# DMA transposes for the last two batches, with the pooled branch added on GpSimd, in an attention and phase-mixing kernel

## The chip, the core and the metric

The kernel runs on one core of a Trainium2 chip. The engines of the core work side by side, each through its own queue in program order: TensorE (PE in the profile) multiplies matrices, VectorE (DVE) and ScalarE (ACT) do elementwise work, GpSimd (POOL) does elementwise work and band masks, and SyncE (SP) issues the DMA transfers. Engines wait for each other through semaphores. The metric is the device time of one execution in microseconds (us); a profiled execution also has a span, from its first to its last instruction.

## The reference

Batch 8, 8 heads, 576 positions, head dimension 64. The attention result has two branches: a pooled one (means over 4 positions, full attention on 144, repeated 4 times) and a local one (a band of 7 positions). Their sum x (576 x 512 per batch) passes a phase-mixing layer.

```python
out_d = sm_attn(q_d, k_d, v_d)                    # q_d, k_d, v_d: means over 4 positions
out_up = np.repeat(out_d, factor, axis=2)
mask = np.abs(pos[:, None] - pos[None, :]) < factor
scores = np.where(mask, scale * np.matmul(q, k.transpose(0, 1, 3, 2)), -1000000000.0)
...
out_local = np.matmul(attn, v)
x = out_up + out_local                            # heads side by side: (B, 576, 512)

theta = x @ w_theta
zr, zi = x * np.cos(theta), x * np.sin(theta)
y = np.einsum('ts,bsd->btd', w_tok_r, zr) + np.einsum('ts,bsd->btd', w_tok_i, zi)
u = x + y
out = u + np.maximum(u @ w_ch, 0.0)
```

## The kernel before

The work of a batch is cut into steps. Each kind of step is a generator that runs over the batches, and each has a letter. The string ORDER (L80) is the program: the loop at L659 takes one letter after the other and lets its generator do its next step. `pin` (L639) then chains the instructions of every engine in just this order, so ORDER fixes each engine's queue, SP's too. No step is moved by anything else.

The steps of a batch, with their letters:

- L `load` (13): four DMAs of q, four of k (each two heads), five of v, into a staging pool of 15 buffers. C `cast` (13): the same to bf16, on GpSimd, for q of batch 0 on ScalarE (`CASTS`, L200). q_tm and k_tm have one buffer each.
- A `turns` (5, L271): for two head pairs of q and k, nine PE transposes each (L285) into a PSUM tile, two ScalarE copies (L287) into qT or kT and a VectorE sum over groups of four positions (L295); the fifth step pools v, with two small products on GpSimd (L310).
- S `scores` (7, L324): two steps of pooled scores, then five chunks of band scores: matmuls (L379), exponential on ScalarE (L387), and two band masks on GpSimd (L394, L396; for batch 0 PE adds a mask, L375).
- N `pooled_out` (3): the pooled branch's result and its transpose xdT. V `outputs` (5): the local branch's psloc (L451), divided by its sums on VectorE into tmp (L460; four buffers).
- T `transposes` (5, L477): four PE transposes of tmp (L487), then VectorE adds xdT, each value for four positions, and writes x transposed, xT (L490).
- H `phases` (5, L500): theta (psth, L507) and its cosine and sine on ScalarE (cs, three buffers, L512 and L513). The fifth step handles the last 64 positions in transposed form (zT, L527); z `z_turn` turns them by a DMA transpose (L535).
- Z `modulate` (4, L540): four PE transposes of xT (L546), then VectorE multiplies them with cs into z (L547).
- X `mix` (5): the matmuls over positions (psu L564, psut L570) and the addition of x (uT, L565). u `u_turn` (2): DMA transposes of uT (L580, L582). R `channels` (5): matmuls with w_ch (psr, L594). O `store` (5): the last elementwise step (osb, L616) and the output DMAs (L622, L625).

Some letters are for set-up: K constants, l and c loads and casts of the weights, W their transposes into WT (L253 copies each result on VectorE), and D, six matmuls on constants that nothing reads (wu, L261), placed in the first 45 us. PSUM is used as two tiles of two banks (`w2`) and four of one (`w1`), taken in turn. Loads, stores and DMA transposes all go through SP's queue.

Of the kernel before, what the change touches and what calls it, by code (L numbers as in the profile page):

```python
# [47 lines left out]
def kernel(  # L48
# [27 lines left out]
    def w1(name, dt=FP32):  # L76
# [1 line left out]


    ORDER = (  # L80
        "LKCLCLLCACLLLLLLKAKCCLLCCCLDKAAlLLlLCCDCSSSCCLLASSLNNLVVllllCllNcCLLVCcCTALLLLLTASCccCcTSCHVVcDTZCCC"
        "ATAHlllHlHZZcHSDZLlLLLLWlccCCCcASSccDzlNCCCSWWWSLNWWCCLLLLLLLLLClCSWCCCCCSWWVAXVANXAACXVXSLTTLLLSuAC"
        "CVSTHTVNHHNLTZZCACCVcLLLLccLcHCCHXzLCZLLSRLLROOZCCCuCLLLLLAARLLLARLSSXCCSCSOOXVVCCCCXSNCVSTAVTCCSROT"
        "ATATCCLLCSXSSHNuHNVXZZAALLCAVHHVCCHNRRzOSSTOCLLCCLLRORLOLLuSCCTZZTSSCHVXVTAHCCNNLXLLZTANAHHLCCVVLLCH"
        "XACACCSLLLLXVXCCzLRSLLLSLLLOTLLLTZZCCSCZATALLuLXSLSHHVNXVNZTXTCAACCCCHHCCHVSuXXRSSROOzCZVNTRRCCSSOOR"
        "AuOuSZZVXVVTTXTLLLSCSCCCHTVXZNAXAAHHVCCHNXZCAHASSRRuROONRuOOSSZTTRSVOzZRSSOTROHVVRRHRSSOOTXOHNTZXNZH"
        "HVXVXXZZzVNVXTTXTHTVHHuuRTRROROOOZZHHzXZZXRXOXXXXXuuRRuROORRuOORORRROOROOO"
    )

    staged = {}  # L90
# [6 lines left out]
    def load(b):  # L97

        for hh in range(4):
            for nm, src in zip("qk", (q, k)):  # L100
                nc.sync.dma_start(
                    out=stage(b, f"{nm}{hh}"),
                    in_=src[b, 2 * hh:2 * hh + 2].rearrange("h (p r) d -> (h p) (r d)", r=WR),
                )
                yield
        for c in range(NCH):
            nc.sync.dma_start(
                out=stage(b, f"v{c}")[0:KW[c], 0:DM].rearrange("p (h d) -> p h d", d=D),
                in_=v[b, :, KS[c]:KS[c] + KW[c], :].rearrange("h p d -> p h d"),
            )  # L110
            yield

    def cast(b):

        q_tm = work.tile([P, 2, WR, 2, D], BF16, tag="q_tm", bufs=1, name=f"q_tm{b}")
        k_tm = work.tile([P, 2, WR, 2, D], BF16, tag="k_tm", bufs=1, name=f"k_tm{b}")
        v_w = v_ws[b % 2]
        inputs[b] = (q_tm, k_tm, v_w)
        eng = CASTS.get(b, CASTS[None])
        for hh in range(4):  # L120
            for i, dst in enumerate((q_tm, k_tm)):
                eng[i](out=dst[:, hh // 2, :, hh % 2, :],  # L122
                       in_=staged.pop((b, f"{'qk'[i]}{hh}")).rearrange("p (r d) -> p r d", d=D))
                yield
        for c in range(NCH):
            eng[2](out=v_w[0:KW[c], c, :, 0:D],  # L126
                   in_=staged.pop((b, f"v{c}"))[0:KW[c], 0:DM].rearrange("p (h d) -> p h d", d=D))
            yield


# [66 lines left out]


    dve, act, gp = nc.vector.tensor_copy, nc.scalar.copy, nc.gpsimd.tensor_copy
    CASTS = {0: (act, gp, gp), None: (gp, gp, gp)}  # L200


    wth = wpool.tile([P, 4, DM], BF16, name="wth")
# [5 lines left out]
    def weight_loads():  # L209

        for i in range(2):
            wst = staged["w", f"th{i}"] = moep.tile([P, 1024], FP32, tag="ur", name=f"th{i}")
            nc.sync.dma_start(out=wst.rearrange("p (c e) -> p c e", c=2),
                              in_=moe_w_theta[256 * i:256 * i + 256, :].rearrange("(c p) e -> p c e", p=P))
            yield
        tail = staged["w", "tail"] = moep.tile([P, 2, S], FP32, tag="xT", bufs=2, name="tail")
        for ri, w in enumerate((moe_w_tok_r, moe_w_tok_i)):
            wst = staged["w", ri] = moep.tile([P, 4, S], FP32, tag="z", name=f"tok{ri}")
            for ct in range(5):
                nc.sync.dma_start(out=wst[:, ct, :] if ct < 4 else tail[0:OC[4], ri, :], in_=w[P * ct:P * ct + OC[ct], :])  # L220
                yield
        for i in range(4):
            nc.sync.dma_start(out=stage("w", f"ch{i}")[:, 0:DM], in_=moe_w_ch[P * i:P * i + P, :])
            yield

    def weight_casts():

        for i in range(2):
            gp(out=wth[:, 2 * i:2 * i + 2, :].rearrange("p c e -> p (c e)"), in_=staged.pop(("w", f"th{i}")))
            yield  # L230
        for ri in range(2):
            for ct in range(5):
                src = staged["w", ri][:, ct, :] if ct < 4 else staged["w", "tail"][0:OC[4], ri, :]
                (gp, dve)[ri](out=w_tm[ri][0:OC[ct], ct, :], in_=src)
                yield
        for i in range(4):
            gp(out=wch[:, i, :], in_=staged.pop(("w", f"ch{i}"))[:, 0:DM])
            yield

    def weight_turns():  # L240

        for j in range(9):
            ps = w1(f"wps{j}", BF16)
            for ct in range(5):
                rows = OC[ct]
                for ri in ((j % 2,) if j < 8 else (0, 1)):
# [3 lines left out]
                        in_=w_tm[ri][0:rows, ct, P * (j // 2):P * (j // 2) + n],  # L250
                        identity=ident[0:rows, 0:rows],
                    )
            nc.vector.tensor_copy(out=WT[:, j, :], in_=ps[:, 0:S])  # L253
            yield

    def warm_up():
# [9 lines left out]
    WARM = ORDER.count("D")  # L266


    parts = {}

    def turns(b):  # L271

        q_tm, k_tm, v_w = inputs[b]
        qT = work.tile([P, 4, S], BF16, tag="qT", name=f"qT{b}")
        kT = kTs[b % 2]
        qdT = work.tile([P, 4, SD], BF16, tag="qdT", name=f"qdT{b}")
# [3 lines left out]
        for j in range(4):  # L280
            n, i = j % 2, j // 2
            tm, To = ((q_tm, qT), (k_tm, kT))[n]
            ps = w2(f"pstr{n}{i}_{b}", BF16).rearrange("p k e -> p (k e)")[:, 0:WR * P]
            for r in range(WR):
                nc.tensor.transpose(out=ps[:, P * r:P * r + P], in_=tm[:, i, r, :, :], identity=ident)  # L285
            for a in range(2):
                act(  # L287
                    out=To[:, 2 * i + a, 0:S].rearrange("p (w r) -> p w r", r=WR),
# [6 lines left out]
                nc.vector.tensor_reduce(out=dst, in_=src, axis=AX.X, op=ALU.add)  # L295
            yield

        vd = vds[b % 2]
        psa, psb = w1(f"psva_{b}"), w1(f"psvb_{b}")
        for c in range(4):  # L300
            nc.tensor.matmul(out=psa[KP * c:KP * c + KP, :], lhsT=PU, rhs=v_w[:, c, :, 0:D],
# [21 lines left out]

    def scores(b):  # L324

        qT, kT, qdT, kdP = parts.pop(b)

        pd = pds[b] = work.tile([P, H + 2, SD], BF16, tag="pd", name=f"pd{b}")
        pms[b] = []

        scale = SCL / 16.0

        def pooled_scores(dst, hh):
# [32 lines left out]
        )  # L366
        yield

        for c in range(NCH):
            kw, qn = KW[c], QN[c]  # L370
            ps = w2(f"psS{c}_{b}")
# [69 lines left out]

    def outputs(b):

        v_w = inputs.pop(b)[2]
        for c in range(NCH):
            kw, qn, cnt = KW[c], QN[c], QC[c]
            ps = w2(f"psloc{c}_{b}")
# [1 line left out]
            for h in range(H):  # L449
# [7 lines left out]
            rl = work.tile([P, 2, 4], FP32, tag="rl", name=f"rl{c}_{b}")  # L457
            nc.vector.reciprocal(out=rl[0:cnt], in_=pv[0:cnt, :, :, 64])
            tmp = tmps[b, c] = work.tile([P, DM], BF16, tag="tmp", bufs=4, name=f"tmp{c}_{b}")
            nc.vector.tensor_tensor(  # L460
                out=tmp[0:cnt].rearrange("p (e j d) -> p e j d", e=2, j=4),
                in0=pv[0:cnt, :, :, 0:D],
# [14 lines left out]
    def transposes(b):  # L477

        xdT = xds.pop(b)
        xT = xTs[b] = moep.tile([P, 4 * S], BF16, tag="xT", bufs=2, name=f"xT{b}")  # L480
        xA, xB = parted(xT)
        for c in range(NCH):
            cnt = QC[c]
            ps = w1(f"xTps{c}_{b}", BF16)[:, 0:512].rearrange("p (e t) -> p e t", e=4)
            tmp = tmps.pop((b, c))
            for dc in range(4):
                nc.tensor.transpose(out=ps[:, dc, 0:cnt], in_=tmp[0:cnt, P * dc:P * dc + P], identity=ident[0:cnt, 0:cnt])  # L487
            for dst, lo, n in ((xA[:, :, QS[c]:QS[c] + cnt], 0, cnt),) if c < 4 else ((xA[:, :, QS[4]:MAIN], 0, MAIN - QS[4]), (xB, MAIN - QS[4], HALF)):
                m = (QS[c] + lo) // 4
                nc.vector.tensor_tensor(  # L490
                    out=dst.rearrange("p e (m j) -> p e m j", j=4),
                    in0=ps[:, :, lo:lo + n].rearrange("p e (m j) -> p e m j", j=4),
                    in1=xdT[:, :, m:m + n // 4].unsqueeze(3).to_broadcast([P, 4, n // 4, 4]),
                    op=ALU.add,
                )
            yield
# [3 lines left out]
    def phases(b):  # L500
# [3 lines left out]
        for c in range(4):  # L504
            th = w1(f"psth{c}_{b}")
            for dc in range(4):
# [1 line left out]
                    out=th, lhsT=xA[:, dc, P * c:P * c + P], rhs=wth[:, dc, :],  # L508
                    start=(dc == 0), stop=(dc == 3),
                )  # L510
            cs = css[b, c] = moep.tile([P, 2, DM], BF16, tag="cs", bufs=3, name=f"cs{c}_{b}")
            nc.scalar.activation(out=cs[:, 0, :], in_=th, func=AF.Sin, bias=pihc, scale=1.0)  # L512
            nc.scalar.activation(out=cs[:, 1, :], in_=th, func=AF.Sin, bias=0.0, scale=1.0)  # L513
            yield
# [25 lines left out]
    def modulate(b):  # L540

        (xA, xB), z = parted(xTs[b]), zs[b]
        for c in range(4):
            ps = w1(f"psxt{c}_{b}", BF16)[:, 0:DM]
            for dc in range(4):
                nc.tensor.transpose(out=ps[:, P * dc:P * dc + P], in_=xA[:, dc, P * c:P * c + P], identity=ident)  # L546
            nc.vector.tensor_tensor(  # L547
                out=z[:, 2 * c:2 * c + 2, :], in0=ps.unsqueeze(1).to_broadcast([P, 2, DM]),
                in1=css.pop((b, c)), op=ALU.mult,
            )  # L550
            yield

# [97 lines left out]
    def batches(steps):  # L650
        for b in range(B):
            yield from steps(b)

    sequences = dict(L=batches(load), C=batches(cast), A=batches(turns), S=batches(scores), N=batches(pooled_out),
                     V=batches(outputs), T=batches(transposes), H=batches(phases), Z=batches(modulate),
                     K=constants(), z=batches(z_turn), u=batches(u_turn), X=batches(mix), R=batches(channels), O=batches(store),
                     l=weight_loads(), c=weight_casts(), W=weight_turns(), D=warm_up())
    pin()
    for s in ORDER:  # L659
        next(sequences[s])  # L660
# [33 lines left out]
```

## Time and profile before

| What | Value |
|---|---|
| Median of 5 runs | 253.4 us (252.87 to 254.29) |
| The profiled execution's own time | 252.99 us |
| Its span | 251.3 us, 6875 instructions |
| Granted TensorE clock, mean | 0.992 |
| DMA: moved, mean | 49.23 MB, 196 GB/s |
| psu (L564): 288 matmuls | 66.9 us busy, 379 ns mean |
| PE transposes of q and k (L285): 144 each | 11.4 and 11.1 us busy |
| PE transposes of tmp (L487): 160 | 14.6 us busy |
| PE transposes of xT (L546): 128 | 11.0 us busy |
| VectorE addition of the pooled branch (L490): 48 | 25.2 us busy, 548 ns mean |
| Table loads on ScalarE | 16, of 1283 ns each |

How to read it: busy time of a group is the time in which at least one of its instructions ran, and "mean" is the length of one. Matmuls are pipelined, so the mean of one is longer than the distance from one to the next. Busy shares are over the whole span; the page also gives them in 40 slices, in tenths. An engine's idle time is shown with what released it.

### The profile page before, as it was taken

The page shows a single profiled execution, that of the slowest core. Times are in us where ns is not written, and L with a number is a line of the kernel's source. Part 1 is how long each engine was busy: PE and PEld are TensorE (multiplying, and loading weights), DVE is VectorE, ACT ScalarE, POOL GpSimd, SP SyncE. Part 2 cuts the span into 40 slices and gives each one's busy share as a digit, 9 for nine tenths or more (in the row PEclk, how much of TensorE's full clock was granted, in tenths as well). Part 3 has the DMA queues.
Part 4 walks back from the last instruction along what each step waited for, and adds up shares of the span by engine and source line. Part 5 has one row for each costly group of instructions (what it writes and reads, how often), then busy time and mean ns, then how long its engine had stood idle before and what let it go on. Part 6 is the DMA issues. An engine that isn't in the chain of part 4 may idle for free.

```text
span 251.3 us, 6875 instructions
## 1 busy us (share of the span) xinstructions
PE 231.2 (92%) x2746; PEld 141.5 (56%) x2746; DVE 193.0 (77%) x357; ACT 159.2 (63%) x245; POOL 152.4 (61%) x211
## 2 busy tenths in 40 slices
PE   0958899999999999979999999999999999999992
PEld 0524555665774567546666666556755556555540
DVE  3444898888898888998989896897989578674363
ACT  4664899645998489959687859547997931520000
POOL 2648663999899999936979953969089410000000
PEclk9997999999999999999999999999999999999999
DMA  6999999999996999449799994762454315041596
GB/s 226 290 297 393 258 225 319 253 230 342 181 182 188 326 189 268 128 118 263 191 352 187 284 255 116 202 131 49 83 181 129 102 24 95 3 167 35 104 263 208
DMA packets 81439, 49.23 MB, mean 196 GB/s; under 512 B 64896, under 2 KB 66944, under 8 KB 81408
## 3 DMA queue, kind: packets, MB, share of 16 engines
q1 hardware_dynamic: 81408, 48.81, 76.6%
q8 instruction: 21, 0.34, 0.6%
q14 instruction: 10, 0.08, 0.2%
HBM read 33.59 MB, written 9.44 MB: 171 GB/s over the span
## 4 chain that ended last, share of the span: by engine, by line
PE 79%; ACT 8%; DVE 4%; DMA 3%; issue 2%; POOL 1%; SPq 1%; DVEq 0%; POOLq 0%; ACTq 0%
PE psu L564 25%; PE psth L507 10%; PE psr L594 7%; PE pstr L285 5%; PE psS L379 5%; PE psloc L451 4%; PE psut L570 3%; PE xTps L487 3%; ACT qT L287 3%; PE psxt L546 3%; DMA out_dram<-osb 2%; ACT kT L287 2%; PE psnd L413 2%; DVE osb L616 2%; PE wu L261 2%
## 5 line engine op out<-in xcount | busy, mean ns | idle before, releaser
L564 PE MATMUL psu<-WT,z 128*128 128x512 bf16 x288 | 66.9, 379 | 0.0
L387 ACT ACTIVATE pm<-psS 128x1024 bf16<-128x1024 f32 (+1 forms) x40 | 38.1, 980 | 15.8 <-PE psS L379 15.6
L394 POOL TENSOR_SCALAR_AFFINE_SELECT pm<-pm 128x1024 bf16<-128x1024 bf16 (+1 forms) x35 | 36.8, 1051 | 12.1 <-ACT pm L387 12.1
L564 PEld LDWEIGHTS <-z 128*128 128x128 bf16 x288 | 26.5, 98 | 27.7
L396 POOL TENSOR_SCALAR_AFFINE_SELECT pm<-pm 128x1024 bf16<-128x1024 bf16 (+1 forms) x35 | 36.6, 1045 | 2.4
L594 PE MATMUL psr<-wch,uT 128*128 128x512 bf16 x128 | 30.7, 379 | 1.5 <-DVE osb L616 1.5
L507 PE MATMUL psth<-wth,xT 128*128 128x512 bf16 x128 | 31.6, 379 | 0.4 <-DVE xT L490 0.4
L565 DVE TENSOR_TENSOR uT<-psu,xT 128x512 bf16<-128x512 f32 x32 | 22.0, 687 | 12.2 <-PE psu L564 12.1
L512 ACT ACTIVATE cs<-psth,pihc 128x512 bf16<-128x512 f32 x32 | 22.6, 707 | 11.9 <-PE psth L507 6.9
L295 DVE TENSOR_REDUCE qdT<-qT 128x288 bf16<-128x1152 bf16 x16 | 21.6, 1351 | 10.6 <-ACT qT L287 10.5
L122 POOL CAST k_tm<-st_k 128x576 bf16<-128x576 f32 x32 | 21.5, 673 | 13.4 <-DMA st_k<-in_k_dram 12.9
L460 DVE TENSOR_TENSOR tmp<-psloc,rl 120x512 bf16<-120x512 f32 (+2 forms) x40 | 27.6, 691 | 1.4
L490 DVE TENSOR_TENSOR xT<-xTps,xdT 128x480 bf16<-128x480 bf16 (+3 forms) x48 | 25.2, 548 | 3.6 <-PE xTps L487 3.6
L126 POOL CAST v_w<-st_v 128x512 bf16<-128x512 f32 (+1 forms) x40 | 23.4, 614 | 5.0 <-DMA st_v<-in_v_dram 5.0
L287 ACT COPY qT<-pstr 128x576 bf16<-128x576 bf16 x32 | 19.0, 647 | 9.8 <-PE pstr L285 9.7
L616 DVE SCALAR_TENSOR_TENSOR osb<-psr,ur 128x512 f32<-128x512 f32 x32 | 21.2, 685 | 3.6 <-PE psr L594 3.1
L295 DVE TENSOR_REDUCE kdP<-kT 128x300 bf16<-128x1200 bf16 x16 | 22.3, 1397 | 2.0 <-ACT kT L287 1.9
L287 ACT COPY kT<-pstr 128x576 bf16<-128x576 bf16 x32 | 19.1, 655 | 6.7 <-PE pstr L285 6.7
L547 DVE TENSOR_TENSOR z<-psxt,cs 128x1024 bf16<-128x1024 bf16 x32 | 21.0, 681 | 1.8 <-PE psxt L546 1.5
L122 POOL CAST q_tm<-st_q 128x576 bf16<-128x576 f32 x28 | 18.9, 673 | 2.5 <-PE psS L379 1.5
L513 ACT ACTIVATE cs<-psth 128x512 bf16<-128x512 f32 x32 | 19.7, 616 | 0.0
L594 PEld LDWEIGHTS <-uT 128*128 128x128 bf16 x128 | 11.5, 98 | 13.5 <-issue 2.1
(86 smaller groups left out, 378.5 us busy)
## 6 DMA issues: line engine op xcount, KB each, us to landing
st_q<-in_q_dram SPq DMA_DIRECT2D x32, 288.0 KB, 5.2
st_k<-in_k_dram SPq DMA_DIRECT2D x32, 288.0 KB, 5.5
st_v<-in_v_dram SPq DMA_DIRECT2D x32, 256.0 KB, 6.4
out_dram<-osb SPq DMA_DIRECT2D x32, 256.0 KB, 2.4
st_v<-in_v_dram SPq DMA_DIRECT2D x8, 192.0 KB, 5.1
tok<-in_moe_w_tok_r_dram SPq DMA_DIRECT2D x4, 288.0 KB, 7.4
tok<-in_moe_w_tok_i_dram SPq DMA_DIRECT2D x4, 288.0 KB, 5.2
th<-in_moe_w_theta_dram SPq DMA_DIRECT2D x2, 512.0 KB, 5.8
```

The lines of the kernel that those rows point to most:

```text
L122: eng[i](out=dst[:, hh // 2, :, hh % 2, :], in_=staged.pop((b, f"{'qk'[i]}{hh}")).rearrange("p (r d) -> p r d", d=D))
L287: act(out=To[:, 2 * i + a, 0:S].rearrange("p (w r) -> p w r", r=WR), in_=ps.rearrange("p (r a w) -> p a w r", r=WR, a=2)[:, a],)
L295: nc.vector.tensor_reduce(out=dst, in_=src, axis=AX.X, op=ALU.add)
L387: nc.scalar.activation(out=pv, in_=ps[0:kw].rearrange("p e (j w) -> p (e j) w", w=P)[:, :, 0:qn], func=AF.Exp, scale=SCL,)
L394: nc.gpsimd.affine_select(out=pv, in_=pv, compare_op=ALU.is_ge, fill=0.0, base=off, pattern=[[0, 8], [-1, qn]], channel_multiplier=1)
L396: nc.gpsimd.affine_select(out=pv, in_=pv, compare_op=ALU.is_ge, fill=0.0, base=6 - off, pattern=[[0, 8], [1, qn]], channel_multiplier=-1)
L460: nc.vector.tensor_tensor(out=tmp[0:cnt].rearrange("p (e j d) -> p e j d", e=2, j=4), in0=pv[0:cnt, :, :, 0:D], in1=rl[0:cnt].unsqueeze(3) ...
L490: nc.vector.tensor_tensor(out=dst.rearrange("p e (m j) -> p e m j", j=4), in0=ps[:, :, lo:lo + n].rearrange("p e (m j) -> p e m j", j=4), ...
L507: nc.tensor.matmul(out=th, lhsT=xA[:, dc, P * c:P * c + P], rhs=wth[:, dc, :], start=(dc == 0), stop=(dc == 3),)
L564: nc.tensor.matmul(out=ps, lhsT=z[:, j, P * dc:P * dc + P], rhs=WT[:, j, 0:MAIN], start=(j == 0), stop=(j == 8))
L594: nc.tensor.matmul(out=psr, lhsT=uA[:, dc, P * c:P * c + P], rhs=wch[:, dc, :], start=(dc == 0), stop=(dc == 3),)
L616: nc.vector.scalar_tensor_tensor(out=osb[:, 0:P * n].rearrange("p (e d) -> p e d", d=P), in0=psr[:, 0:P * n].rearrange("p (e d) -> p e d", ...
```

## The change

In batches 6 and 7 (`DMA_QK`, `DMA_X`, `DMA_Z`):

- q and k are turned by four DMA transposes (`turn_qk`, letter q) of 128 x 1152 into staging buffers; the ScalarE copies then read those.
- tmp is turned by five DMA transposes (`turn_x`, letter t) of 128 x 512, also into staging buffers. The rows of tmp that a chunk does not fill are set to zero on GpSimd before. GpSimd, not VectorE, adds xdT.
- xT is turned by one DMA transpose of 128 x 2048 (`turn_z`, letter x), and the multiplication for z reads that.

In all batches: steps are cut finer (loads and casts of v, letters v and w; pooled v, B; pooled scores, Q, apart from the band scores, S; w_ch, h and g), cs has four buffers in place of three, five of the nine copies into WT are on ScalarE, v is always cast on GpSimd, and ORDER is another string.

```diff
-        "LKCLCLLCACLLLLLLKAKCCLLCCCLDKAAlLLlLCCDCSSSCCLLASSLNNLVVllllCllNcCLLVCcCTALLLLLTASCccCcTSCHVVcDTZCCC"
...
+        "KLLLLCCLLKKKLCALCvCvvCCCDvvLLwLLAALLAlvlllSSLwLSwwwVBCCCCQQVNNlllAVcNvvvCTTAcvcTllCCSSHHVVDTTlllALHc"
...
-    CASTS = {0: (act, gp, gp), None: (gp, gp, gp)}
+    CASTS = {0: (act, gp), None: (gp, gp)}
...
-            nc.vector.tensor_copy(out=WT[:, j, :], in_=ps[:, 0:S])
+            (act, dve)[j % 2](out=WT[:, j, :], in_=ps[:, 0:S])
...
+    DMA_QK, DMA_X, DMA_Z = (6, 7), (6, 7), (6, 7)
+
+    def turn_qk(b):
+
+        if b in DMA_QK:
+            q_tm, k_tm = inputs[b]
+            for j in range(4):
+                t = turned[b, j] = stg.tile([P, WR, P], BF16, tag="st", name=f"qk{j}_{b}")
+                nc.sync.dma_start_transpose(out=t, in_=(q_tm, k_tm)[j % 2][:, j // 2].rearrange("p r h d -> p (r h d)"))
+                yield
+
+    def turn_x(b):
+
+        if b in DMA_X:
+            for c in range(NCH):
+                t = turned[b, "x", c] = stg.tile([P, 4, P], BF16, tag="st", name=f"xt{c}_{b}")
+                nc.sync.dma_start_transpose(out=t, in_=tmps.pop((b, c)))
+                yield
+
+    def turn_z(b):
+
+        if b in DMA_Z:
+            xA, xB = parted(xTs[b])
+            t = turned[b, "z"] = moep.tile([P, 16, P], BF16, tag="xr", bufs=1, name=f"xr_{b}")
+            nc.sync.dma_start_transpose(out=t, in_=xTs[b][:, 0:4 * MAIN])
+            yield
...
-            ps = w2(f"pstr{n}{i}_{b}", BF16).rearrange("p k e -> p (k e)")[:, 0:WR * P]
-            for r in range(WR):
-                nc.tensor.transpose(out=ps[:, P * r:P * r + P], in_=tm[:, i, r, :, :], identity=ident)
+            if b in DMA_QK:
+                ps = turned.pop((b, j)).rearrange("p r w -> p (r w)")
+            else:
+                ps = w2(f"pstr{n}{i}_{b}", BF16).rearrange("p k e -> p (k e)")[:, 0:WR * P]
+                for r in range(WR):
+                    nc.tensor.transpose(out=ps[:, P * r:P * r + P], in_=tm[:, i, r, :, :], identity=ident)
...
+            if b in DMA_X:
+                lo = 96 if c < 4 else 64
+                nc.gpsimd.memset(tmp[lo:], 0.0)
...
+            if b in DMA_X:
+                ps = turned.pop((b, "x", c))
+            else:
...
+            adder = nc.gpsimd if b in DMA_X else nc.vector
...
-                nc.vector.tensor_tensor(
+                adder.tensor_tensor(
...
-            cs = css[b, c] = moep.tile([P, 2, DM], BF16, tag="cs", bufs=3, name=f"cs{c}_{b}")
+            cs = css[b, c] = moep.tile([P, 2, DM], BF16, tag="cs", bufs=4, name=f"cs{c}_{b}")
...
+            if b in DMA_Z:
+                ps = turned[b, "z"][:, c:16:4, :]
+            else:
...
-                out=z[:, 2 * c:2 * c + 2, :], in0=ps.unsqueeze(1).to_broadcast([P, 2, DM]),
-                in1=css.pop((b, c)), op=ALU.mult,
+                out=z[:, 2 * c:2 * c + 2, :].rearrange("p r (e d) -> p r e d", d=P),
+                in0=ps.unsqueeze(1).to_broadcast([P, 2, 4, P]),
+                in1=css.pop((b, c)).rearrange("p r (e d) -> p r e d", d=P), op=ALU.mult,
```

In the new ORDER the end of the program, from the first mixing step of batch 6 on, reads `XXTttTTuTTXHHRHxROOROuROZHZHRZzZOXXuXXXXuRuRROOOXRRRuOORRROOOORO`; before it read `XTTXTHTVHHuuRTRROROOOZZHHzXZZXRXOXXXXXuuRRuROORRuOORORRROOROOO`.

## The prediction

> **What bounds the kernel now.** I read the page's busy rows and slices first, then the chain of waits, then what TensorE (PE) waited for between 60 and 240 us.
>
> ```profile
> PE 231.2 (92%) x2746; PEld 141.5 (56%) x2746; DVE 193.0 (77%) x357; ACT 159.2 (63%) x245; POOL 152.4 (61%) x211
> ...
> PE   0958899999999999979999999999999999999992
> ...
> POOL 2648663999899999936979953969089410000000
> ...
> PE 79%; ACT 8%; DVE 4%; DMA 3%; issue 2%; POOL 1%; SPq 1%; DVEq 0%; POOLq 0%; ACTq 0%
> ```
>
> PE is above 90% from the sixth slice (6.3 us each) to the last but one; only the start and the end have holes. GpSimd (POOL) is empty from slice 34 on.
>
> ```profile
> PE psr L594 <- DVE osb L616: 1.5, 1, 1.5
> PE psloc L451 <- ACT qT L287: 0.5, 2, 0.4
> PE psS L379 <- ACT qT L287: 0.4, 1, 0.4
> PE psS L379 <- ACT kT L287: 0.3, 1, 0.3
> PE xTps L487 <- DVE osb L616: 0.2, 1, 0.2
> ```
>
> The columns are waiter, what it waited for, total us, times, longest. Five rows, 2.9 us in 180: for most of the span the end is set by how much PE has to do. A change that takes work from PE is paid in full, one that takes it from another engine is not, unless it makes PE wait.
>
> **PE: what goes.** Batches 6 and 7 lose the turns of q and k (per batch 4 steps of 9), of tmp (5 of 4) and of x (4 of 4). The groups' busy means (225, 216, 219 ns for one turn) overlap, so I take start-to-start times from the order of time on PE (start, length, engine, line):
>
> ```profile
> 55.76 0.67 PE L285 MATMUL pstr<-ident,q_tm 128*128 128x128 bf16 x9
> 56.26 0.67 PE L285 MATMUL pstr<-ident,k_tm 128*128 128x128 bf16 x9
> ...
> 63.39 0.38 PE L487 MATMUL xTps<-ident,tmp 120*128 120x120 bf16 x4
> 63.61 1.03 PE L507 MATMUL psth<-wth,xT 128*128 128x512 bf16 x4
> ...
> 221.30 0.61 PE L546 MATMUL psxt<-ident,xT 128*128 128x128 bf16 x8
> 221.75 1.03 PE L507 MATMUL psth<-wth,xT 128*128 128x512 bf16 x4
> ```
>
> Nine turns take 0.50 us (55.76 to 56.26), four of tmp 0.22, eight of x 0.45. Per batch 4 x 0.50 + 4 x 0.22 + 0.17 (the short chunk, 33.76 to 33.92) + 0.90 = 3.95, for two batches **7.9 us**. By the groups' busy totals (79, about 91 and 86 ns each) it would be 12.1; I choose 7.9, since the next group starts before the last one's modelled end.
>
> **A rule that speaks against it.** The Trainium skill, "VectorE: DVE Perf Modes", section "The three transpose paths", gives 390 ns for a 128x128 turn on TensorE and 1309 ns by DMA, and its rules take TensorE where the result may lie in PSUM. 144 blocks (72, 40, 32) at 0.92 more each would be 132 us lost, if each stood on the path. The trace differs in what counts: a block holds PE for 0.056 us, and a DMA turn holds PE for nothing. I go by the trace, and ask which DMA turn is waited for.
>
> **The DMA turns.** Twenty are added: 8 of 128x1152 (295 KB), 10 of 128x512 (131 KB), 2 of 128x2048 (524 KB). The trace has the second size as z (landing 2.4/2.6/7.4 us min/median/max) and the third as ur:
>
> ```profile
> L535 SPq DMA_TRANSPOSE z<-zT x8: 1191/1270/2965, 42.0 to 225.2; - x8
> ...
> DMA to landing us min/median/max: 2.4/2.6/7.4
> ```
>
> ```profile
> L580 SPq DMA_TRANSPOSE ur<-uT x8: 1317/2370/4905, 62.4 to 237.8; - x8
> ...
> DMA to landing us min/median/max: 4.3/4.5/7.0
> ```
>
> So 131 KB cost 1.3 us of SP and 2.6 to land, 524 KB 2.4 and 4.5; 295 KB lie between, some 3.4 to land. SP gains 8 x 1.7 + 10 x 1.3 + 2 x 2.4 = 31 us, the DMA engines 4.7 MB. Loads and stores queue behind a turn on SP: the q and k turns of 6 and 7 sit among the loads of 6 and 7, whose casts come over 10 us of PE later; from 200 to 240 us the DMA share is 0.16 to 0.49. Bounds 0 to 3 us, taken at 0 apart from the two places below.
>
> **GpSimd, VectorE and ScalarE.** The add L490 takes DVE 3 x 0.647 + 0.668 + 0.412 + 0.265 = 3.3 per batch; DVE loses 6.6, which PE does not see. On POOL the nearest row is vd at L310 (two inputs, 256 elements, median 614 ns, 2.4 ns each): 480 elements 1.15, a batch 5.5, two 11.0. The ten memsets of tmp rows lie between a 103 ns POOL memset and a 673 ns cast; I take 0.3, 3 us in all. POOL's order from the fourth band select of batch 6 to the last add of batch 6 holds the selects of six band steps (12.6), vd of 7 (1.2), one cast (0.6), memsets (0.9) and adds (5.5): 20.8 us. PE has 24.8 from that step to the fourth phase step of batch 6, which needs the add. It fits by 4 us, less the exponential (1.03) that POOL trails by. Each memset also stands before DVE's write of tmp in rows both touch; behind that wait are psu's evictions. Five of nine WT copies go to ACT (0.45 on DVE, 0.65 like the other copies): 3 us on an engine full from 30 to 40 us, 0 to +2 at the start. The copies L287 now read SBUF; nearest row 0.65 in PSUM, taken the same, 0 to +0.1 each.
>
> **The second rule, and the place where it costs.** The Trainium skill, "SBUF — State Buffer", section "Who interferes with whom": a VectorE instruction with two SBUF inputs contends with a GpSimd one that reads SBUF, and the later one is blocked until the other finishes. The multiply z (L547) now has two SBUF inputs. This trace has one such DVE operation, zT:
>
> ```profile
> 105.75 3.01 DVE L527 TENSOR_TENSOR zT<-xT,cst 128x512 bf16<-128x512 bf16 x1 [0.18 <-ACT cst L525]
> ```
>
> Beside POOL's back-to-back vd and casts it took 3.01 us instead of 0.43, and the PE wait of 1.5 us above follows it. By the rule a multiply waits out one POOL instruction (1.15 at most): 4 for batch 6 is 4.6. By this row it is 2.6 each, 10.3, since POOL got in again. At batch 7 POOL's queue is empty. Between 0 and 10.3 I take the rule's 4.6: POOL's order has three adds and a select beside the four. From the eviction X5.0 to psu X6.0, PE has some 14.3 us and DVE 10.3, so 4 are covered. In that stretch x6's turn also stands on the way: last add of batch 6, turn 4.5, four multiplies 2.7, together 7.2, against 6.8 of PE work from the fourth phase step to psu of batch 6. The uncovered 0.6 and 0.4, and half a us for POOL's trail: **+1.5 us**, bounds 0 and 6.
>
> **The end.** For batch 7, after its last psloc PE has psu and psut of 5 and psu of 6 (8.8), then phases, psr of 5 and the rest of 6 (10.9): 19.7 us to psu of 7. Beside it: tmp 1, turn issue and landing 3.9, add 0.9, x turn 4.5: 10.3, earlier than the fourth phase (14.8). After the tail phase (16.2): ACT to 17.9, zT 18.4, z's turn 21.0; its matmul is psu's ninth, at 21.4. No wait. The last stores keep their order: 0.
>
> **The start, and batches 0 to 5.** The same work in another order.
>
> ```profile
> 16.05 0.30 PE L335 MATMUL psSd<-qdT,kdP 64*128 64x144 bf16 x4 [1.94 <-DVE kdP L295]
> ...
> 17.27 0.59 PE L375 MATMUL psS<-band,ident 128*128 128x512 bf16 x2 [0.69 <-ACT pd L345]
> ```
>
> The band scores of batch 0 waited for the pooled ones (1.94 + 0.69); they now come first and need only kT, about 14.4. By 50 us ACT's phases and tables bind both orders, so I keep 1.0 of the 2.6: **-1.0**, bounds -3.5 and +3. The table changes between exponential and sine stay at 15. Moved loads count the same: v behind q and k. The cs buffers rise from 3 to 4, for four phases before the first multiply of batch 6.
>
> **Sum.** The profiled execution took 252.99 (span 251.3 and 1.7 around it): 252.99 - 7.9 - 1.0 + 1.5 = 245.6. The shown median is 0.4 above that execution: **246.0**.
>
> **Rivals.**
> - A, the waits don't come and the start gives its 3.5: 252.99 - 7.9 - 3.5 + 0.4 = 242.0. For it: PE waited little before. Against: ACT at 9.4 of 10 from 30 to 40 us.
> - B, POOL and DVE block each other as at 105.75: +6 at psu of batch 6 instead of 1.5, 250.5. For: that row. Against: the same operation at 182.05 took 0.42 with vd beside it.
> - C, slower: the turns land late. At 7.4 and 7.0 instead of 2.6 and 4.5, and an SP held 4.9 by a ur turn, batch 7's multiplies end at 25.7 instead of inside 19.7 (+6), and batch 6's at 1.5 + 4.8 + 2.5 = +8.8: 252.99 - 7.9 - 1.0 + 14.8 + 0.4 = 259.3. It decides once added waits pass 8.9. For: the queue's packets take 76.6% of the engines. Against: late in the trace that share is half or less.
> - That PE keeps the turns is excluded by the diff; that they cost nothing is what the 2.9 us of waits deny.
>
> **Chances.** Forecast 0.50, A 0.12, B 0.16, C 0.22. Runs spread so that 0.3% (0.76 us) can be told from no change. Of B 0.03 and of C 0.04 fall inside it: faster 0.75, same 0.07, slower 0.18. The range of the forecast alone is 243.5 to 248.5; 241.5 to 255 leaves out a little of A and most of C's far half.
>
> **What would show it.** Right: PE's matmul count down by 144, PE above 90% in the same slices, psu of batch 7 starting without a wait. Wrong: PE waiting for z before psu of batch 6 or 7 (B: z much longer than 0.68; C: z idle on a DMA turn), for xT on POOL before psth, or PE holes before slice 25, where only the order changed.

## The result, and the profile after

The changed kernel takes 251.98 us (median of 38 runs, 250.58 to 255.74) against 253.25 us for the kernel before (73 runs on the same chips, 252.30 to 255.16). The ratio is 0.9957, with a 95% interval of 0.9945 to 0.9969: 1.1 us faster, where 7.4 were forecast. Medians are of all runs; ratios leave out single slow ones, over 1.5% above the fastest of their kernel. The profiled execution took 251.82 us, 1.17 less than the one before.

The page of the kernel after, in the rows and slices that were shown of before (now 6.25 us a slice), with the shares of the chain of waits:

```profile
PE 225.1 (90%) x2602; PEld 135.9 (54%) x2602; DVE 185.0 (74%) x340; ACT 170.1 (68%) x250; POOL 167.4 (67%) x233
...
PE   0878799799999989999999999999769999999991
...
POOL 4538773996999999979679576996498972600000
PEclk9997999999999999999999999999988999999997
...
PE 69%; ACT 12%; POOL 6%; DVE 4%; DMA 4%; issue 2%; SPq 0%; DVEq 0%; ACTq 0%; POOLq 0%
```

PE has its 144 matmuls fewer. But slices 29 and 30, at 175 to 187 us, are now 7 and 6 tenths, and PEclk falls to 8 in slices 30 and 31. VectorE (DVE) lost 8.0 us of work; ScalarE (ACT) gained 10.9 and GpSimd (POOL) 15.0. The part of the chain on PE fell from 79% to 69%; ScalarE and GpSimd took it over.

The three longest of PE's waits between 60 and 250 us, kernel after (waiter, what it waited for, total us, times, longest):

```profile
PE psvb L347 <- POOL v_w L131: 2.2, 1, 2.2
PE psr L650 <- DVE uT L621: 1.4, 1, 1.4
PE psloc L496 <- DVE tmp L508: 0.5, 1, 0.5
```

All three are new. The first two lie in that hole. The third comes at 204.6 us, behind a write of tmp that VectorE could not start, because GpSimd had yet to zero the empty rows:

```profile
203.88 0.69 DVE L508 TENSOR_TENSOR tmp<-psloc,rl 120x512 bf16<-120x512 f32 x1 [1.53 <-POOL tmp L507]
```

None of the three is a wait for z or for a DMA transpose.

To place the loss I take the PE work that the program puts between two steps (start-to-start times, as in the prediction) from the time that PE took for it. The steps are the X steps; X4.3 is the fourth mixing step of batch 4, X5.0 the first of batch 5. In the kernels with the new order X5.0 is counted from the last matmul ahead of it (195.33 us; psu itself starts at 195.44), so that this matmul's 0.1 us is in neither the time nor the work. The table compares one execution of each kernel.

| Stretch | After minus before, us |
|---|---|
| PE work in all (222.9 to 214.9) | -8.0 |
| lost time up to X3.0 (20.9 to 19.8): start, new order | -1.1 |
| lost from X3.0 (133.8) to X4.3 (173.0) | +1.1 |
| lost from X4.3 to X5.0: 22.3 taken for 16.9 of work; before 24.4 for 24.3 | +5.3 |
| lost from X5.0 (195.3) to X5.3 (207.6) | +0.8 |
| the rest: end of the program (0.4), rounding | +0.7 |
| change of the span (251.3 to 250.1) | -1.2 |

The PE work saved is there, to 0.1 us of what was forecast. Most of it is lost again in one stretch, from 173 to 195 us, in which batch 6's scores, batch 7's turns and batch 4's last steps meet.

**What happens there.** The granted clock and the busy times of the engines, kernel after (stretch, us, busy us and instructions of PE, PEld, DVE, ACT, POOL, then PEclk, DMA share, GB/s):

```profile
170.00:180.00 10.00, 8.61 (x99) 4.77 (x98) 7.38 (x13) 9.32 (x12) 3.98 (x8) 1.00 0.94 154
180.00:190.00 10.00, 7.80 (x102) 4.66 (x100) 5.44 (x11) 3.95 (x6) 9.44 (x13) 0.83 0.70 184
```

First ScalarE is full and GpSimd stands still; ten us later it is the other way round. ScalarE's groups by form say what fills it (instructions, busy us, mean ns, idle time before them):

```profile
L328 ACT COPY kT<-pstr 128x576 bf16<-128x576 bf16 x24 | 14.4, 660 | 2.4 <-PE pstr L326 2.4
L328 ACT COPY qT<-pstr 128x576 bf16<-128x576 bf16 x24 | 14.2, 647 | 11.3 <-PE pstr L326 11.2
...
L328 ACT COPY kT<-qk 128x576 bf16<-128x576 bf16 x8 | 9.4, 1238 | 0.0
L328 ACT COPY qT<-qk 128x576 bf16<-128x576 bf16 x8 | 9.2, 1208 | 0.0
...
L507 POOL MEMSET tmp<- 32x512 bf16 x8 | 3.9, 520 | 0.2
...
L263 ACT COPY WT<-wps 128x576 bf16<-128x576 bf16 x5 | 3.2, 639 | 3.0 <-PE wps L258 3.0
```

One more row, of the kernel before: the casts of q of batch 0, which ScalarE reads from SBUF in order.

```profile
L122 ACT CAST q_tm<-st_q 128x576 bf16<-128x576 f32 x4 | 2.6, 678 | 2.3 <-DMA st_q<-in_q_dram 2.3
```

The same copy takes 0.65 us from the PSUM tile pstr and 1.22 from the SBUF tile qk. Reading 576 values in order takes 0.64 from PSUM (WT) and 0.68 from SBUF (the casts of q, in float32). So neither the tile in SBUF nor the step of 256 bytes is slow alone; the two together are. Sixteen such copies at 0.57 more are 9 us of ScalarE; five copies of WT are most of the rest of its gain. The memsets take 0.52, not 0.3.

The four queues in order of time at that place (start, length, engine, line, what it does; in brackets the idle time before and what ended it). ScalarE:

```profile
173.99 2.36 ACT L328 COPY kT<-qk 128x576 bf16<-128x576 bf16 x2
176.37 1.28 ACT L432 ACT_TABLE_LOAD   x1
177.66 1.69 ACT L432 ACTIVATE pm<-psS 128x1024 bf16<-128x1024 f32 x2
```

VectorE:

```profile
176.38 1.40 DVE L336 TENSOR_REDUCE kdP<-kT 128x300 bf16<-128x1200 bf16 x1 [1.75 <-ACT kT L328]
177.70 1.28 DVE L621 TENSOR_TENSOR uT<-psu,xT 128x512 bf16<-128x512 f32 x2
```

GpSimd:

```profile
178.75 1.09 POOL L439 TENSOR_SCALAR_AFFINE_SELECT pm<-pm 128x1024 bf16<-128x1024 bf16 x1 [5.89 <-ACT pm L432]
...
181.88 0.85 POOL L441 TENSOR_SCALAR_AFFINE_SELECT pm<-pm 96x736 bf16<-96x736 bf16 x1
182.79 0.98 POOL L507 MEMSET tmp<- 32x512 bf16 x2
183.83 0.61 POOL L131 CAST v_w<-st_v 96x512 bf16<-96x512 f32 x1
```

PE:

```profile
178.44 2.75 PE L650 MATMUL psr<-wch,uT 128*128 128x512 bf16 x12 [1.40 <-DVE uT L621]
...
184.49 0.24 PE L347 MATMUL psvb<-v_w,pu 96*32 96x128 bf16 x4 [2.20 <-POOL v_w L131]
```

Read together: batch 7's last k copies end at 176.3. By then two queues stand behind them. VectorE waits 1.75 us with its sum kdP, and behind the sum stands the eviction uT, for which PE waits 1.40. On ScalarE itself the exponentials of batch 6 (pm) come behind the copies and a table load of 1.28; GpSimd has waited 5.89 us for them, then does four selects, two memsets and only then the cast of v, for which PE waits 2.20. The holes are followed by a stretch of 3.4 us at half clock in the PEclk record: four psr matmuls at 188.03 took 1.46 us instead of 1.03. Half of 3.4, an estimate, is 1.7 us more. 1.4 + 2.2 + 1.7 are 5.3 of the 5.4 lost.

### The profile page after: what moved, and what is told of

Its sections match the earlier page's. It is cut to its first block, busy times and chain, and to the rows that moved or that the text cites. A ratio compares the mean times of both kernels' runs of the same rounds, so it can differ in the third digit from the quotient of the medians.

```text
span 250.1 us, 6628 instructions
## 1 busy us (share of the span) xinstructions
PE 225.1 (90%) x2602; PEld 135.9 (54%) x2602; DVE 185.0 (74%) x340; ACT 170.1 (68%) x250; POOL 167.4 (67%) x233
## 2 busy tenths in 40 slices
DMA packets 100511, 53.94 MB, mean 216 GB/s; under 512 B 83968, under 2 KB 86016, under 8 KB 100480
## 3 DMA queue, kind: packets, MB, share of 16 engines
q1 hardware_dynamic: 100480, 53.53, 90.9%
## 4 chain that ended last, share of the span: by engine, by line
PE 69%; ACT 12%; POOL 6%; DVE 4%; DMA 4%; issue 2%; SPq 0%; DVEq 0%; ACTq 0%; POOLq 0%
PE psu L620 23%; PE psth L559 8%; PE psr L650 7%; PE pstr L326 5%; PE psloc L496 4%; PE psS L424 4%; ACT pm L432 3%; ACT kT L328 3%; PE psut L626 3%; PE xTps L538 2%; ACT qT L328 2%; DMA out_dram<-osb 2%; POOL pm L441 2%; PE psxt L601 2%; POOL pm L439 2%
## 5 line engine op out<-in xcount | busy, mean ns | idle before, releaser
L336 DVE TENSOR_REDUCE kdP<-kT 128x300 bf16<-128x1200 bf16 x16 | 22.3, 1396 | 4.8 <-ACT kT L328 4.6
L328 ACT COPY qT<-pstr 128x576 bf16<-128x576 bf16 x24 | 14.2, 647 | 11.3 <-PE pstr L326 11.2
L496 PEld LDWEIGHTS <-pm 128*128 128x128 bf16 (+1 forms) x320 | 14.6, 104 | 7.5 <-issue 1.4
L542 DVE TENSOR_TENSOR xT<-xTps,xdT 128x480 bf16<-128x480 bf16 (+3 forms) x36 | 18.3, 548 | 0.5 <-PE xTps L538 0.4
L496 PE MATMUL psloc<-v_w,pm 128*128 128x65 bf16 (+1 forms) x320 | 16.5, 198 | 1.8 <-ACT pd L386 0.6
```

Source lines behind the costliest of these rows:

```text
L328: act(out=To[:, 2 * i + a, 0:S].rearrange("p (w r) -> p w r", r=WR), in_=ps.rearrange("p (r a w) -> p a w r", r=WR, a=2)[:, a],)
L496: nc.tensor.matmul(out=pv[0:qn, h // 4, h % 4, :], lhsT=pms[b][c][0:kw, 4 * par + blk, 0:qn], rhs=v_w[0:kw, c, h, 0:65], start=(h % 4 == 0 ...
```

## The experiments

My theory after the comparison was the **copies**: sixteen ScalarE copies grew from 0.65 to 1.22 us, and those of batch 7 come late. The rivals: **GpSimd**, whose new memsets and adds make its queue late by themselves; and the **order**, which would lose the time whatever the steps cost. "Stretch" below is X4.3 to X5.0, 22.3 us in the kernel after. All edits are to the kernel after unless said otherwise, and line numbers are its own. All of these kernels compute the whole output.

**Another access order for the copy.** The copy reads with a step of 256 bytes and writes in order. Here it reads in order and writes with a step of 9 elements (18 bytes).

```diff
-                act(
-                    out=To[:, 2 * i + a, 0:S].rearrange("p (w r) -> p w r", r=WR),
-                    in_=ps.rearrange("p (r a w) -> p a w r", r=WR, a=2)[:, a],
-                )
+                dst, src = To[:, 2 * i + a, 0:S], ps.rearrange("p (r a w) -> p a r w", r=WR, a=2)[:, a]
+                if b in DMA_QK:
+                    act(out=dst.rearrange("p (w r) -> p r w", r=WR), in_=src)
+                else:
...
```

> The 16 ScalarE copies of q and k of batches 6 and 7 read the turned tile in order and write with a step of nine elements, in place of reading with a step of 256 bytes and writing in order. Copy theory (the copies out of SBUF take 1.21 us in place of 0.65, ScalarE runs 9 us late, and GpSimd and PE wait behind it from 173 to 196 us): the copies fall to about 0.65 to 0.7, ScalarE's busy time by some 8 us, PE's waits in that stretch go, 246 to 248 us against 252. GpSimd theory (memsets, adds, casts and selects in one queue make PE wait): copies shorter, time 251 to 252. If a step on the write side costs as much as on the read side, copies stay near 1.2 and the time at 252, and this run tells nothing about PE's wait.

Measured: 278.63 us, 1.0979 (1.0942 to 1.1016). The copies became slower, not faster. Groups by form of this kernel:

```profile
L330 ACT COPY kT<-qk 128x576 bf16<-128x576 bf16 x8 | 21.9, 2996 | 0.0
L330 ACT COPY qT<-qk 128x576 bf16<-128x576 bf16 x8 | 21.6, 2958 | 0.0
```

Sixteen copies at 1.75 more are 28 us of ScalarE, and the time grew by 26.6. As a cure it missed. It shows that the end follows these copies when they are slow enough. It doesn't measure the 5.4 us: most of the new loss lies ahead of the stretch (X3.0 to X4.3 took 62.1 us instead of 39.2, the stretch 24.9 instead of 22.3), where batch 6's copies are.

Is it the tile in SBUF or the step of the write? In the kernel before, the same edit for batches 6 and 7, with PSUM as the source:

```diff
+                if b >= 6:
+                    act(out=dst.rearrange("p (w r) -> p r w", r=WR), in_=src)
```

> The kernel before, with the 16 ScalarE copies of batches 6 and 7 reading PSUM in order and writing SBUF with a step of nine elements. If the write step made the copies of 2.97 us in the first run, these take about 3 us too; if reading from SBUF did, they stay near 0.65 to 1.2.

Measured (one run): 290.24 us. Groups by form:

```profile
L289 ACT COPY kT<-pstr 128x576 bf16<-128x576 bf16 x8 | 21.9, 2997 | 0.7 <-PE pstr L285 0.7
```

The write with a step costs 3.00 us from PSUM too; there the source makes no difference. With the step on the reading side it does: 0.65 against 1.22. (16 x 2.3 = 37 us of copies, and the time is 36.6 us above the 253.66 of the kernel before on that chip.)

**q and k back on PE.**

```diff
-    DMA_QK, DMA_X, DMA_Z = (6, 7), (6, 7), (6, 7)
+    DMA_QK, DMA_X, DMA_Z = (), (6, 7), (6, 7)
```

with the letters q taken out of ORDER.

> q and k of batches 6 and 7 are turned on PE again; x and z stay on DMA. PE gets 4.0 us of work back. Copy theory: the loss of 5.6 us between X of batch 4 and X of batch 5 goes, time 249 to 251 us. GpSimd theory: the loss stays and PE's work is added, 255 to 256 us.

Measured: 261.28 us, 1.0280 (1.0239 to 1.0321). The copies were 0.65 again, and the stretch fell to 17.5, as the copy theory asks. But some 7 us were lost elsewhere: from X3.0 to X4.3 PE took 50.5 us instead of 39.2 (4 of it work), waiting 3.3 us in pstr for PSUM tiles that VectorE still read. This order was made for turns that use no PSUM. Counted from X3.0, PE also came to the stretch 11.3 us later than in the kernel after, which gave the other engines time to catch up. So the run agrees with the copy theory in the stretch, does not prove it there, and decides nothing about the total.

**x back on PE**, its addition back on VectorE, without the memsets; letters t out of ORDER, six buffers of tmp.

```diff
-    DMA_QK, DMA_X, DMA_Z = (6, 7), (6, 7), (6, 7)
+    DMA_QK, DMA_X, DMA_Z = (6, 7), (), (6, 7)
...
-            tmp = tmps[b, c] = work.tile([P, DM], BF16, tag="tmp", bufs=4, name=f"tmp{c}_{b}")
+            tmp = tmps[b, c] = work.tile([P, DM], BF16, tag="tmp", bufs=6, name=f"tmp{c}_{b}")
```

> The attention result of batches 6 and 7 is turned on PE again and the pooled branch added on VectorE, without memsets; tmp gets six buffers, since the order needs them. q, k and z stay on DMA. PE gets 2.1 us back, GpSimd loses 15 us. GpSimd theory: the loss between X of batch 4 and X of batch 5 goes, 248 to 249 us. Copy theory: most of the loss stays, 252 to 255 us, and the copies stay at 1.2 us.

Measured: 254.66 us, 1.0036 (1.0008 to 1.0064); the stretch is 21.1. Taking the adds and memsets off GpSimd did not close it, and PE still waited 1.4 us for uT: against GpSimd as the only cause. The total is no clean test, as PE has its 2.1 us of turns back and new waits at psu, 0.9 for xT and 0.7 for z's DMA.

**Only the memsets gone.** tmp's four buffers are made once, with their empty rows zeroed at the start by VectorE.

```diff
+        t = const.tile([P, DM], BF16, name=f"tmp_buf{i}")
+        nc.vector.memset(t[64:], 0.0)
...
-            if b in DMA_X:
-                lo = 96 if c < 4 else 64
-                nc.gpsimd.memset(tmp[lo:], 0.0)
+            tmp = tmps[b, c] = tmp_bufs[(NCH * b + c) % 4]
```

> The rows of tmp that a chunk does not fill are set to zero once, at the start, in four lasting buffers, in place of ten memsets on GpSimd. GpSimd theory: VectorE no longer waits for the memsets (4.0 us in all in the profile after), nor the cast of v behind them, and the time falls to 248 to 250 us. Copy theory: GpSimd idles 5.9 us for ScalarE anyway, so at most 1 us, 251 to 252 us.

Measured: 249.45 us, 0.9828 (0.9793 to 0.9863); the stretch is 19.8. The copy theory allowed at most 1 us and missed; this is the gain that the GpSimd theory named. PE's wait for the cast of v fell from 2.2 to 1.1, since two memsets (0.98 us) no longer stood ahead of it; the wait of 1.4 for uT stayed, and no half clock follows in this trace. Behind the stretch, from X5.0 to the end, the kernel takes 54.0 us instead of 54.7; the eight further ones below with lasting buffers and all three turns on DMA take 53.9 to 54.2. So neither cause is the whole.

**Half of the slow copies to another engine.** If the sum of ScalarE's work counted, moving the second copy of each pair should take most of the rest. Five placements: to VectorE or GpSimd, for both batches or batch 7 alone; f1, f2, g1 and g2 stand on the kernel with lasting tmp buffers, f4 on the kernel after.

```diff
-                act(
+                ((dve) if a and b in DMA_QK else act)(
```

> On top of the run with the memsets made once: of each turned q or k tile of batches 6 and 7 VectorE copies the second half, ScalarE the first. ScalarE loses 8 x 1.21 = 9.7 us. Two causes in series (late ScalarE copies, then memsets in GpSimd's queue): with both gone PE keeps its pace from X of batch 4 to X of batch 5 (about 17.5 us in place of 22.3), 246 to 247.5 us. If the memsets alone were the cause, or if VectorE's copies cost as much as they save, 249 to 251 us.

> The same with the second half copied on GpSimd in place of VectorE. GpSimd idled 5.9 us while it waited for ScalarE, so eight copies of batch 7 and 6 at some 0.7 to 1.2 us would fit there: 246 to 249 us; if they stand before casts and selects that PE waits for, 250 to 253 us.

> The changed kernel with the second half of each turned q or k tile copied on VectorE, memsets left as they are. Series theory: it takes away the late ScalarE and most of the loss, 247 to 249.5 us. If the memsets are the cause, 251 to 252 us as without it.

(`gp` in place of `dve` in f2 and g1; `b in (7,)` in g1 and g2.)

> Memsets made once, and GpSimd copies the second half of the turned q and k tiles of batch 7 alone (of batch 6 it cost some 2.5 us of PE waits before X of batch 4 in the last runs). Series theory: X of batch 4 to X of batch 5 at about 17 us in place of 19.8, nothing lost before: 246 to 247.5 us. If what GpSimd takes on comes back later as waits for selects, 249 us.

> The same with VectorE for the second half of batch 7. VectorE is the one that holds back psr by uT here (1.4 us, 1.8 with the split of both batches), so less is won: 247.5 to 249.5 us; at 246 to 247 us VectorE had room after all.

| Kernel | Second copy on | Stretch, us | Median, us | Ratio to before |
|---|---|---|---|---|
| memsets once, no split | - | 19.8 | 249.45 | 0.9828 (0.9793 to 0.9863) |
| f1 | VectorE, 6 and 7 | 18.8 | 251.39 | 0.9924 (0.9891 to 0.9956) |
| f2 | GpSimd, 6 and 7 | 17.1 | 249.15 | 0.9846 (0.9810 to 0.9882) |
| g1 | GpSimd, 7 | 18.3 | 251.73 | 0.9941 (0.9912 to 0.9970) |
| g2 | VectorE, 7 | 18.8 | 250.50 | 0.9879 (0.9850 to 0.9908) |
| f4 (after, memsets kept) | VectorE, 6 and 7 | 18.9 | 252.49 | 0.9951 (0.9923 to 0.9979) |

The stretch shrank each time, down to 17.1 for 16.9 of work. The time did not follow. A copy took 1.17 us on GpSimd and 0.64 to 1.54 on VectorE, and held up what stood behind it there: from X3.0 to X4.3 f1 took 42.4 us and f2 41.6 instead of 39.2, and in g1 PE waited 2.2 us at once for a PSUM tile that VectorE had yet to read. All of these expectations missed the total as the copy theory had it, f2 by 0.15 us; f4 lies half a us above what its expectation gave to the memsets as the cause. The best of them, f2, equals the lasting buffers alone. They show that the hole can be filled, and that this is not the way. They do not show that the copies' time is what was lost, since PE came to the stretch 1.6 to 3.2 us later in all five, counted from X3.0.

**z back on PE**, on g1, with the letters x out of ORDER: what is the third turn worth?

```diff
-    DMA_QK, DMA_X, DMA_Z = (6, 7), (6, 7), (6, 7)
+    DMA_QK, DMA_X, DMA_Z = (6, 7), (6, 7), ()
```

> The kernel of g1 with x of batches 6 and 7 turned on PE again (32 turns in 8 steps). If a PE turn costs what lies from start to start (0.056 us) and PE binds there, 1.8 us more than g1; by busy time (0.086 us) 2.75; 0 if the place has slack.

Measured: 255.90 us, 1.0085 (1.0054 to 1.0117), 4.2 us more than g1. The 1.8 us of PE work come back, and beyond that PE waits 0.7 for cs at pstt, 0.7 for z's own DMA and 0.4 for cs at psu. In that kernel this part of the change pays in full, and more.

**The place of the late copies.** Now every instruction stays as it is, and one step is moved: A7.3, the turn step of k's second half in batch 7 (two copies and the sum kdP). If its place counts, the exponentials and uT should each be freed by moving it behind them. First behind the last band scores of batch 6, S6.4: h1 on the kernel after, h2 with lasting tmp buffers, h3 with A7.2 moved as well.

```diff
-...VVAHvwwwHtAtwXSSXXRRRRuu...
+...VVAHvwwwHttwXSSAXXRRRRuu...
```

> The changed kernel with one letter of ORDER moved: the last turn step of batch 7 (two copies of 1.2 us on ScalarE, and the sum of four on VectorE) stands behind the last two band-score steps of batch 6, in place of before them. Nothing is removed. Theory of the queue (the slow copies cost time where they stand ahead of the exponentials that GpSimd, then PE wait for): those exponentials start 2.4 us earlier, uT's eviction no longer waits for the sum, X of batch 4 to X of batch 5 takes 18 to 20 us in place of 22.3, time 248 to 250. If ScalarE's total time binds, the place makes no difference: 252.

> The same with the memsets made once at the start. Both causes of the theory out of the way of PE: 17 to 18 us from X of batch 4 to X of batch 5 in place of 19.8, and 246.5 to 248.5 us. By total ScalarE time: 249.5, as with the memsets alone.

> As before, with the last two turn steps of batch 7 moved. 4.8 us of copies out of the way; the pooled scores of batch 7 come later and may wait for the sums: 246 to 249 us. By total ScalarE time: 249.5.

Measured: 253.22 (0.9957, 0.9931 to 0.9984), 252.55 (0.9957, 0.9929 to 0.9985) and 253.25 us (0.9982, 0.9957 to 1.0006). All three expectations missed, and the stretch grew, to 23.4, 23.3 and 24.0 us. On the kernel after the move gained nothing (the ratio is the same, the median 1.2 us higher); on the lasting buffers it lost 3 us. PE's waits and VectorE's order of time in h2:

```profile
PE psr L653 <- DVE uT L624: 3.5, 1, 3.5
```

```profile
181.46 1.40 DVE L342 TENSOR_REDUCE kdP<-kT 128x300 bf16<-128x1200 bf16 x1 [4.12 <-ACT kT L334]
182.78 0.68 DVE L624 TENSOR_TENSOR uT<-psu,xT 128x512 bf16<-128x512 f32 x1
```

The exponentials came first now and the wait for v was gone from PE's list, but the sum still stood ahead of uT, and waited 4.12 us instead of 1.75. One of the two queues was freed and the other paid. In h3 the wait for uT is 4.5. So the step has to go behind the eviction as well: behind X4.4, the last step of batch 4 that writes uT (i1: `XSSXXARRRR`), or further, behind V6.3 (i2; and i3, the same letter in the kernel after, with its memsets).

```diff
-...HtAtwXSSXXRRRRuuOOONOVtVzwTB...
+...HttwXSSXXRRRRuuOOONOVtVAzwTB...
```

> Memsets made once; the last turn step of batch 7 stands behind the last mixing step of batch 4 (X4.4), so behind the evictions of uT in VectorE's queue as well as behind the exponentials in ScalarE's. Two-queue theory (the late copies reach PE by VectorE's sum in front of uT, which h1 made worse, and by the exponentials in front of GpSimd's selects): PE no longer waits for uT, 17 to 18.5 us from X of batch 4 to X of batch 5 in place of 19.8, 247 to 248.5 us. If only the total of ScalarE counts: 249.5.

> The same, with the step further back, behind the fourth output step of batch 6 and the osb steps of batch 3. Two-queue theory: as the run before or better, 246.5 to 248.5 us, unless the pooled scores of batch 7 now wait for this sum (249 to 251).

> The changed kernel with that one letter moved behind the fourth output step of batch 6 and nothing else changed: no work is removed from any engine. Two-queue theory: 248 to 250 us against 252, the difference to the run before being the memsets. If ScalarE's total time binds: 252.

Measured: i1 250.54 us, 0.9872 (0.9824 to 0.9920), stretch 21.0, with a new wait of 1.8 in psxd and a dip of the clock. i2 **247.72 us, 0.9776 (0.9739 to 0.9813)**, stretch 18.7: faster than both kernels. i3 250.97 us, 0.9891 (0.9863 to 0.9920), stretch 20.1. What PE waited for in i2, the longest first:

```profile
PE psS L430 <- ACT kT L334: 0.6, 1, 0.6
PE psS L430 <- ACT qT L334: 0.5, 2, 0.3
PE psS L430 <- ACT pm L438: 0.4, 1, 0.4
PE psS L430 <- ACT pd L392: 0.4, 1, 0.4
PE psvb L353 <- POOL v_w L131: 0.4, 1, 0.4
```

No wait above 0.6, and the clock stayed at 1.00 from 160 to 200 us. i2 landed in its forecast range, i1 and i3 some 2 and 1 us above theirs. In i3, where nothing but one letter's place differs from the kernel after, the wait for uT is gone, and 1.6 for v and 3.4 us of half clock are left. Against 0.9957 for the kernel after, the place alone is worth 0.7% (1.7 us by 0.0066 x 253). Lasting buffers alone are worth 1.3%, both together 1.8%. The intervals of i2 and of the lasting buffers alone overlap, so the place on top of the buffers rests on the traces: from X3.0 to the end they take 116.3 us (kernel after), 114.0 (i3), 113.2 (buffers alone) and 111.9 (i2).

## Why the prediction was wrong in size

It had the direction and the mechanism of the gain. Of the eight points below four stood, and a fifth hit its number by luck. Two terms that failed carry the shortfall, both of them costs on engines other than PE.

- **PE's work**: forecast -7.9, measured -8.0. The start-to-start times were the right choice; the busy totals would have given 12.1.
- **The start**: forecast -1.0, measured -1.1 by X3.0. The number is luck. Up to X0.0, where I had put the gain, the lost time rose by 1.5 us (X0.0 started at 52.0 instead of 50.8, and lies at 51.6 to 54.5 in five traces of kernels that are the same up to there). The gain, 2.6, came from X0.0 to X3.0, where I had put none; 1.5 of it is before's wait for osb, which is gone (I had read over it in the PE row, where slice 18 stands at 7 tenths). The sign that I had named, PE holes before slice 25, did show: slices 8 and 15 stand at 7 and 8 tenths, both at 9 before.
- **The DMA turns** were never waited for by PE. Those of q and k landed later than forecast (5.1 us median, not 3.4; the queue's share of the engines rose from 76.6% to 90.9%), with room to spare. Rival C did not come.
- **The multiply z beside GpSimd**: +1.5 forecast, 0 measured. All eight took 681 to 686 ns, and none waited. But they did not run beside GpSimd's work: in its order of time the last addition of batch 6 ends before 201.6, the first multiply starts at 206.28, and until 209.7 GpSimd does one memset of 0.53. The DMA turn between them reads all of xT but its last 64 positions, so those additions of the batch must be over by then, which I could have seen in the diff. So neither the row at 105.75 nor the rule weighed beside it (the Trainium skill, "SBUF — State Buffer", "Who interferes with whom") was put to the test, and rival B could not come.
- **The end**: no wait for z before psu of batch 7, as forecast.
- **GpSimd's additions**: 0.995 us for 480 elements, forecast 1.15.
- **The first term that failed** is the sentence "The copies L287 now read SBUF; nearest row 0.65 in PSUM, taken the same, 0 to +0.1 each". Measured: +0.57 each, 9 us on ScalarE. I moved the source of an instruction from PSUM to SBUF and kept its price, though no row of the trace showed a copy from SBUF with a step. Its bounds should have been wide.
- **The second** is GpSimd's queue. I let it trail the exponentials by 1.03 us in the fit ("It fits by 4 us, less the exponential") and by half a us in the sum. PE's fourth band step of batch 6 starts at 172.50 and its first select at 178.75, 6.25 us later: the exponentials came behind the slow copies, and GpSimd stood idle for 5.89. The memsets (0.52, not 0.3) were ahead of the cast of v, which I had counted in the queue without asking who waits for it. And I named their other wait ("Each memset also stands before DVE's write of tmp") but gave it nothing: VectorE waited 4.0 us for them in all. Without the memsets the kernel is 1.3% faster, some 3.3 us of 253.

Of the 6.2 us between 245.6 and the profiled 251.82, the stretch from X4.3 to X5.0 is 5.4. The rest is 0.8 just behind it (0.7 of it goes with the memsets), the 1.1 lost before it and 0.4 at the end, less the 1.5 that z did not cost.

That the memsets and the place of the late turn step cause most of the loss is shown by taking each away, e4 and i3, and both, i2, which is 4.6 us by ratio below the kernel after. That the copies' slowness is what makes the place matter is shown in part: slower copies cost more (e1, g3), and with copies of 0.65 the stretch closes (e2), but there PE came late; no run changed the 0.57 alone. That the dip of the clock follows from the holes is only read from the traces, and the length of a hole doesn't settle it: i2 has neither holes nor dip from 160 to 200 us, e3 (1.4 and 0.8) and e4 (1.4 and 1.1) have holes and no dip, f2 has a hole of 2.1 and none, i3 one of 1.6 and a dip. No run set a hole by itself. Also open: a layout in which the SBUF copy is as fast as from PSUM was not tried, and about 2 us of the stretch remain in i2.

## What to carry to other kernels

When a change gives an instruction another source or another access step, price it as a new instruction, from where it reads and the step on the reading and on the writing side. Then look along each engine's queue for what stands behind the instruction that became slow, and behind those that wait for it: here a sum that nobody needed soon was queued ahead of an eviction that PE needed at once. Part of that loss was mended by moving one step. Work given to a free engine may well be late on the path: here ten short memsets on GpSimd cost at least as much as the place of that step.

## What the hardware showed

- A ScalarE copy of 128 x 576 bf16 took 0.65 us from PSUM with a read step of 256 bytes (0.64 in order), 1.22 from SBUF with the same step, and 3.0 when it wrote with a step of 18 bytes, from either. On VectorE the copy from SBUF took 0.64 at its shortest, on GpSimd 1.17.
- GpSimd set 32 x 512 bf16 to zero in 0.52 us and 64 x 512 in 0.53: twice the rows took no longer.
- Two holes of PE, 1.4 and 2.2 us within 8 us, were followed by half clock for 3.4 us; so was a single hole of 1.6 us (i3), but not one of 2.1 (f2).
- DMA transposes come in small packets: 4.7 MB more moved on the queue came with 19,072 more packets (100,480 against 81,408), some 250 bytes each.
